# Sixteen exponential tiles, a V bank drawn per unit from all eight, one tile for gate and product, and a new order table

## The chip, the cores and the metric

The kernel runs on one core of a Trainium2 chip. The metric is the device time of one execution in microseconds (us). Before the change three runs took 1710.9, 1711.95 and 1711.96 us, so the median is 1711.95 us.

## What is computed

The input x has 2048 tokens of 512 numbers. It is normalised by a layer norm without weights to xn. One branch is full attention with 32 heads of 16 numbers each; the other is a bilinear gated feed-forward network of hidden width 1792. The output joins them.

```python
xn = layernorm(x)
q, k, v = split(xn @ wqkv)                     # 32 heads of 16
p = softmax(q @ k.T * 16 ** -0.5)              # 2048 x 2048 a head
s = (p @ v) @ wo
b = ((xn @ w_gate) * (xn @ w_up)) @ w_down     # 512 -> 1792 -> 512
out = x + s * silu(b)
```

All data are float32. Products other than p @ v split each operand into a high and a low float32r part and add three partial products, so they keep float32's precision.

## The kernel before, in words

**Units and steps.** Attention is cut into 32 units: eight groups of four heads (from line 887 on) by four chunks of 512 queries. A unit has 16 steps, one for each block of 128 keys. In a step `expo` (line 952) makes, for each of the four heads, one matmul of scores (128 keys by 512 queries, line 955) into a PSUM bank, and ScalarE (ACT) writes its exponentials to an SBUF tile `e` (line 957). When the four tiles of a step are there, `pv` (line 960) multiplies them with V (line 966): four matmuls of 128 rows by 32 columns, one for each head, each in a quarter of the bank `pv`, which adds up the 16 steps of its unit. Each of these float32 matmuls stands twice in the trace, so a step is eight records.

**Maxima.** The softmax needs each query's maximum over the keys. `score` (line 922) makes the scores a second time in the other layout (128 queries by 512 keys, line 927), and VectorE (DVE) reduces each bank to a maximum (line 929). There are 2048 such banks and 2048 of exponentials.

**Two halves of the array.** Score, exponential and all other products of the main part (the projections to q and k, gate, up, down and output products, line 465) use 48 to 64 rows of TensorE. A matmul in the lower half of the rows (0 to 63) runs beside one in the upper half. A product of 128 rows is done as a low part in the lower half and then a high part in the upper half; between them ACT reads one number of the bank (`look`, line 500), which holds the high part back until the low part has ended. The V products use all 128 rows and so have TensorE to themselves. A *batch* below is a run of V products without another matmul in it; a *stretch* is what stands between two batches.

**The order table.** The order on TensorE (PE), ACT and DVE is written out as a string, `ORDER`, and class `Order` (from line 470) reads it code by code:

- `t`/`T` one exponential, `s`/`S` one score block, each in the lower/upper half; the digit behind it is the PSUM bank
- `o` with a bank opens an output and makes its first low product, `f` makes a further low product, `F` a high product
- `v`, `w`, `z` one, two or three steps of V products
- `l` the look at a finished low part; `e` an output's copy by ACT, `d` one by DVE; `h` the split of a hidden block; `x`, `c`, `b` the three DVE pieces that read a unit's finished bank, divide by the sums and turn the result back; `m`, `r` the maxima of a unit; `k` the copies of turned tokens; `Q` the load of finished heads for the last product

Instructions that GpSimd (POOL) and the DMA queue (SP) get are put in order by the framework behind the mark `|`.

**Buffers.** `etile` (line 228) rotates through EBUFS = 14 tiles `e`, that is three and a half steps. PSUM has eight banks: seven with digits, and the eighth, tag `pv`, for the V products of every unit in turn. `pv` draws that bank anew where a unit begins (line 963), so the first V product of a unit waits until DVE has read the unit before (`first` in `heads`, line 993). The copies of q and k go through `qr` (three tiles, ACT writes, line 300) and `hl` (two tiles, POOL writes the high part, line 309); both are then stored to DRAM. In the feed-forward part ACT copies a gate block to `g` (line 683), DVE multiplies it with the up block into `h` (line 688), ACT writes the high part `hh` (line 434) and POOL the low part `hl` (line 435).

Of the kernel before, what the change touches and what calls it, by code (L numbers as in the profile page):

```python
# [41 lines left out]
2FfFfS5fFmfFfFfFs1Flo3S6efFfFs2FfFfFfFfFfS5fFfFfFrfS1o0FlfFs6FefFs2FfFfFs5FfFfFfS1fFfS6fFfFo4S2lfFs5FefFfFfFs1FfFfFs6F
fFfFfS2fS5fFo3FlfS1efFfT6s2Ft5T0fFfFfS1fS6t2Fs5FfFfT0fS1fFo2FlfT6s0FfT5fFs1FfFes6Ft0T5fFfFs1Ft4Fs6Ft0FfFfS5t1FfS4fFs6F
fS0et1T5lzs4T3s6Ft1Fo0FfT5s3FfT4fS1t6FfFfS5s3FfT4fFt6Fs1FfT5s4FfT3fS6fFt5S1lwet3S4s6T5t2Fo1FfFs3Ft4Fs5FfFt6S2fFfT3fS4f
T5fS6fFt2S3fFfFfFs4S5let2S6zo3T0s4FfT2fS5t6FfFs0Ft4FfS2t5FfFfT6s0FfFfS4fT5fT2s6FfFs0Flt5T4wemrt2S6s0Ft5Fo4FfT1fS2t6FfF
s0Fs5T1fFt2FfS6fFt1FfS0fT5fFfFfS6es2S1lt0S5wt3S6s2Ft0Fo1FfT5s3FfT6fFs2T0fFfT5fS3fT6fFs2T0fFt5Fs3FfFs6Fs2S0ewfT5o3S6lfT
4fS2fT0s5FfFt6Fs4Ft2Ft0FfFfT6s5FfFs4FfT2fFfT0s5FfS6s4S2elwxt0Fs5Ft1Ft6Fo4S2fT0fFfS5fT1fS6fT2fFfS0t5Fs1Ft6FfFfFs0Fs2S5e
fS1zlct6T3s0Ft2Fo5S1fFfT6fFfS0t3Ft1FfS2fFs6FfT0t3FfFfS2fT1fS6s0Fls3Fwes2T1t4T6s0Fo3FfFfS1fFfT2s0T4fFfS6t1FfT2fFt0S4fFs
6FfFfFs1Fls4T2t0Ft6Fwebt2S1t0Ft6Fs4Fo5FfT2fS1fFfT0fS4t6FfFt2S1fFt0FfS4fFmfS6es1S2zrfT0o4S6lfT3fS1fT2fFs0Ft6Ft3Fs1FfFt2
Fs0Ft6FfFs1T3fT2fFfS0fFt6T1fT3wels0T2o6T1fS3fFt5Fs2FfFfT0s3FfT1fS5t2FfFs0Ft3Fs1Ft5S2fFfFfS0efS3s1S5lzs2T4s0Ft3Fo1FfT5f  # L50
S4t2FfS3t0FfFs5Ft4FfT2s3FfFfS0fT4s5FfFfS3efS2t4T0lvxt6T4t0Fs5Ft3T2wct6S5t4S0t3Fo2FfFfS6fT5fS4fT0s3FfFfT6s5FfT4fFfFs3Ff
Fs5S0les6T4zs3T1o5T4t0S6fFfFfS1fT3s4FfT6fFt0Fs1FfFt3S4t6FfFs0FfT1fT3s4Ft6FwebfS0o1S4lfT3fFt6FfS2t0FfFs4Ft3FfS6t2Fs0FfF
t3S4fFfT6fFfFfS0es2T3lt4S6ws0T5s2Fo3T4fT6fFfS5fT0fS4mfFt2T6fFfS5s0Ft4FfFs2Ft6FfFfFs5Fls0S4et6Fzrt1S2s5Ft6Fo0T4fFfS1t2F
s6FfFfT5fS4fT1s2FfT6fT5fFs4FfFfT1wls2Fs4Fet6T5o1FfFfS3t2FfS6t4FfFfS5t3FfS2t6Fs4FfFfT3fFfFfS5es2T6ls4T3wxt0Fs5Ft6Fs2Ft3
Fs4Fo0Ft5FfS6t2FfFfS3fT5fS4fT6fFfFfS3efS2fS5t6T4lwct1S3s2T6t4Fo5FfFs1FfT3fS6fT2fFs4FfT1s3Ft6FfFfS2t1Fs4FfFfS3efS6s2S1l
zt0S4t3S6o2T1fFfFs0Ft4Fs3FfT6fFs1FfT0fT4s3FfFfS6fT0fT1fFt4Flbs3Ft0S6wet1S3t4Ft0Fo6S5fFfS1fT3fFfT4s5FfT0fT1s3FfFs4Ft5Fs
0FfFs3T1fFt5S4zdhmrfT1o0S3lfT5fS4fT2fFs1Ft3Ft5Fs4Ft2FfFs1FfFfT3fS4t5FfS2fFt3FfS1t4S5lwet3S2s1Ft4Fo5T6fFs3Ft2FfFfS1s4T6
fFfT3fS2fFfT6s1FfT4s3FfFfFs2S6lt4T1zdht4S3t1Fs2Fo6FfT0fS4fT3fS1fT2fS0fFfT4s3Ft1FfFfS2t4Fs0FfFs3Flt1Fs2T4vexs0T1s3Ft4Ft
5S2wct1S0s3T4t5Fo2FfFfS1fT0fS4fT3fS5fFt1FfS0fT4fFs3Ft1Fs5FfFs0T4lwdhs3T1s5T4t0Fo6FfFfS1fT3fS4t5FfFs0FfT1s3Ft4FfFs5Ft1T
0fFfS4fS3fFs5T1lzebt0S4t1T2o3S5fFfFfS0fT4fS1fT5fFs2FfT0s4Ft1FfFs5Ft0Fs2FfFt1T4fFs5S0lwds2T1t4T5s0Fo6FfFfS1fFfT2s0Ft4Ff  # L60
S5t1FfFfS2t0FfS4hmt5FfFs1FfS2fT0welrt5S4s1Ft0T3o2FfFfS5fT4s0FfT1fFs3Ft5Fs4Ft0FfS1fFfT5fFfS3s4FfS0s1T5lzdht5S3s4Ft0Fo1F
fT6fS5t3FfT0fS4fFfT6fS5t3FfFt0S4fFs6FfT5s3FfFt0Flt4s6S5wexs3T0t4Fs6T2o5FfFs0Ft3FfFt4Fs6FfT2fS0fT3fFs4FfT6fS2fT0fS3fFfS
4fFfS6s2S0lzcds3T4t6Fs2Fs0Ft1Fs4Ft3Ft6Fo2FfFt1FfS0fT3fT4fS6fFs1FfT0fT3fFfS6fT4fS1fFfFs0S3let6S4ws1T5t6Fs0Ft3Ft4Ft5Fs1F
t6Ft0Fwbs1T3o4T5s6FfFfT0fS3fT1fFfS6fT5fS0fT3fFs1Ft5FfS6fFfS0efT3s1S5lwmt2S6t3Fs0T1o5FfFs2FfT6s3FfT0fS1fFt2FfS6t3Ft0FfF
s1T2rfFfFs6FfFfFfS1efS3fS0s6S2lzt4S1t3Ft0S6o2FfFfS4fT1s3Ft6FfFfS0fT4t1Fs3FfT6fFt4S0fFfFs3T1fFs6Fls0Ft4Fhs3T1zes6T4s0Ft
1Ft5Ft3Fs4Fs6Ft1Fo0FfT5fT4fS3fFfS6fFt1Fs5FfT3fS4fT6vext1T3t6S5t2T4wcfS5fT1o3S6lfS2fT4fT5s1FfFt6Fs4FfFt5Fs2Ft6T1fFfFfS4
fFfS2fFs5S6ls1Ft4Fzdhs2T4t5Fs6Fs1Ft0Ft4Fo2FfS5fT6fT0fFfS1t4FfT5s6FfFfT0fFbfS1fT4s6S5lwes1T0s6Ft4Fs5Ft3Ft0Ft1Fo4FfS6fFf
S3fT5fS0fFfT1fS6fT5fFs3FfFs0S1lt5T6wds3T5t6T0s1Fo2FfFfS5fT3fFt6S1fS0mfFt5Ft3FfFfS1t6FhfS0t5FfFfFs1S3lwers0T6t5Fs1Ft4Ft
3Fs6Fo0FfS5fT1fFfS4fT6fT3fS5fFfS1t6Fs4FfFs5S3fFs1S6lzds4T5s3T1o6T2fFfFfS5fT4fFt1S3fFfT2fS5t4FfFs3T1fFt2Fhs5FfFt4Flt1Fw
ext2T4s3Fs5T1o0FfFfS2fFt3Fs4FfT5t1FfFs2FfT3fS4fT5fFfS1fFt3Fls2S4zcdhs1T5s2T3o4T6fFfFs5FfFt1Fs2T3fFfS6fT5s1FfFt2Ft3FfS6  # L70
fFfFfS1et5S2lt3S6wt0S1t5T3o2S6fFfFfS0fT1fS5fT6fFfT3s0FfFt1S5fT6fFs3Ft0FfS1fFfFs5Fls3Fs6Fs0T1zbdt1S5t3Fo6S0fT4fFs1Ft5Fs
# [1058 lines left out]
```

## Time and profile before

| what | value |
| --- | --- |
| median of three runs | 1711.95 us |
| the profiled execution, whole | 1711.76 us |
| its span, first to last instruction | 1708.6 us |
| PE busy | 1695.8 us (99%) |
| DVE busy | 1440.7 us (84%) |
| ACT busy | 1221.5 us (71%) |
| POOL busy | 583.7 us (34%) |
| DMA | 145.80 MB, mean 85 GB/s |

The profile is of one execution. Its span leaves out 3.2 us that lie around the first and last instruction. A row of a timeline gives start, duration, engine, line, operation, output<-inputs, shapes and how many instructions were merged into it; a bracket gives the idle time of the engine before it and what ended it. Matmuls are pipelined, so a matmul's row is longer than the distance to the next one; pace is read from starts.

### The profile page before, as it was taken

What the parts mean: (1) busy time and instruction counts of PE and PEld (TensorE: products, weight loads), DVE (VectorE), ACT (ScalarE), POOL (GpSimd) and SP (SyncE); (2) the same over time, 40 slices, a digit from 0 to 9 for tenths busy, and PEclk for the clock granted to TensorE, in tenths of its full rate; (3) what the DMA queues carried; (4) which work ended last, traced back from release to release, by engine and by line L of the source; (5) the groups of instructions that cost most, each with busy time, mean ns of one, the idle gap of its engine ahead of it and who ended that gap; (6) DMA issues with size and microseconds to landing.
All of it is one profiled execution on the core that took longest, in us unless ns stands there. A gap on an engine that the chain in (4) does not pass through costs nothing.

```text
span 1708.6 us, 35418 instructions
## 1 busy us (share of the span) xinstructions
PE 1695.8 (99%) x13792; PEld 1089.4 (64%) x13792; DVE 1440.7 (84%) x2464; ACT 1221.5 (71%) x2503; POOL 583.7 (34%) x618
## 2 busy tenths in 40 slices
...
PEclk9999999999999999999999999999999999999999
...
DMA packets 119794, 145.80 MB, mean 85 GB/s; under 512 B 12620, under 2 KB 74060, under 8 KB 116940
## 3 DMA queue, kind: packets, MB, share of 16 engines
...
## 4 chain that ended last, share of the span: by engine, by line
PE 97%; DVE 1%; POOL 1%; issue 0%; DMA 0%; ACT 0%; POOLq 0%; SPq 0%; DVEq 0%
PE b L465 37%; PE pv L966 27%; PE b L955 16%; PE b L927 15%; PE v L354 1%; PE p L354 0%; DVE mx L929 0%; DMA ks<-in_x_dram 0%; POOL dh L770 0%; PE b L332 0%; POOL y L441 0%; PE xT L317 0%; POOL hl L769 0%; ACT ks L295 0%; POOLq L1122 0%
## 5 line engine op out<-in xcount | busy, mean ns | idle before, releaser
L929 DVE TENSOR_REDUCE mx<-b 128x1 f32<-128x512 f32 x2048 | 1278.3, 683 | 186.4 <-PE b L927 99.3
L957 ACT ACTIVATE e<-b 128x512 f32<-128x512 f32 x2048 | 1084.1, 603 | 362.8 <-PE b L955 194.2
L927 PE MATMUL b<-ks,qs 48*128 48x512 f32 x2048 | 751.6, 412 | 0.0
L955 PE MATMUL b<-qs,ks 50*128 50x512 f32 x2048 | 722.4, 414 | 0.2
L966 PE MATMUL pv<-e,V 128*32 128x512 f32 x4096 | 488.4, 598 | 0.0
L955 PEld LDWEIGHTS b<-qs,ks 50*128 50x128 f32 x2048 | 342.4, 184 | 159.4 <-issue 48.6
L927 PEld LDWEIGHTS b<-ks,qs 48*128 48x128 f32 x2048 | 357.5, 184 | 131.6 <-DVE mx L929 51.0
L966 PEld LDWEIGHTS pv<-e,V 128*32 128x32 f32 x4096 | 109.0, 109 | 233.5 <-issue 223.6
L465 PE MATMUL b<-fh,w1h 64*128 64x512 f32 x504 | 199.4, 398 | 0.4 <-ACT look L500 0.4
L465 PE MATMUL b<-fl,w1h 64*128 64x512 f32 x504 | 197.4, 394 | 0.0
L465 PE MATMUL b<-fh,w1l 64*128 64x512 f32 x504 | 197.1, 393 | 0.0
L247 POOL CAST w1h<-w1r 128x512 fp32r<-128x512 f32 x60 | 36.6, 610 | 468.3 <-DMA w1r<-in_wg_dram 261.5
L465 PE MATMUL b<-fh,w0h 64*128 64x512 f32 x500 | 196.4, 395 | 0.0
L465 PE MATMUL b<-fl,w0h 64*128 64x512 f32 x500 | 195.7, 393 | 0.0
L465 PE MATMUL b<-fh,w0l 64*128 64x512 f32 x500 | 195.5, 393 | 0.0
L465 PE MATMUL b<-dh,hh 64*128 64x512 f32 x448 | 160.8, 396 | 0.0
L465 PE MATMUL b<-dh,hl 64*128 64x512 f32 x448 | 158.2, 394 | 0.0
L465 PE MATMUL b<-dl,hh 64*128 64x512 f32 x448 | 157.3, 393 | 0.0
L247 POOL CAST w0h<-w0r 128x512 fp32r<-128x512 f32 x60 | 36.6, 611 | 206.3 <-DMA w0r<-in_wu_dram 109.0
L465 PEld LDWEIGHTS b<-fh,w1h 64*128 64x128 f32 x504 | 92.9, 185 | 11.2 <-issue 2.2
L465 PEld LDWEIGHTS b<-fh,w1l 64*128 64x128 f32 x504 | 93.1, 185 | 8.8 <-issue 3.4
L465 PEld LDWEIGHTS b<-fl,w1h 64*128 64x128 f32 x504 | 93.3, 186 | 5.1 <-issue 0.8
...
## 6 DMA issues: line engine op xcount, KB each, us to landing
...
KD<-hl SPq DMA_DIRECT2D x16, 512.0 KB
QD<-hl SPq DMA_DIRECT2D x16, 512.0 KB
...
```

The costliest lines, as they stand in the source:

```text
L247: cast = nc.gpsimd.tensor_copy(hi, raw)
L354: nc.tensor.matmul(o, l(d), r(d), start=k == d == 0, stop=k == 2 and d == ND - 1)
L465: nc.tensor.matmul(self.o, l[rows], r[rows], start=x == 0 and n == 0, stop=last and (x == 0 or self.engine is not None), skip_group_check= ...
L927: nc.tensor.matmul(o, QS[i][b:b + KB, pr, t * P:(t + 1) * P], k[b:b + KB, pr, kc * 512:(kc + 1) * 512], start=True, stop=True)
L929: nc.vector.tensor_reduce(MX[i][:, j, t, kc:kc + 1], o, axis=AX.X, op=OP.max)
L955: nc.tensor.matmul(o, k[b:b + KR, pr, kt * P:(kt + 1) * P], QS[i][b:b + KR, pr], start=True, stop=True)
L957: fst["recent"] = fst["exp"] = nc.scalar.activation(e, o, AF.Exp, scale=DH ** -0.5).ins.name
L966: nc.tensor.matmul(fst["pv"][32 * j:32 * j + 32], V[:, kt, h0:h0 + 32], es[j], start=kt == 0, stop=kt == NT - 1)
```

## The change

The number of exponential tiles goes from 14 to 16, which is four whole steps. At the same time `qr` has two tiles in place of three, `hl` has one in place of two, and the product of gate and up block is written over the gate block, in tile `g`; tile `h` is gone. (At the very end `last_heads` took `h` for a low part; it now takes `e2`.)

The bank of V products is no longer a fixed one. A new code `P` with a digit draws any of the eight banks for the next unit and puts it in `pvs`; scores, exponentials and outputs may use digit 7 too. A unit's V products so write another bank than the one that DVE reads for the unit before, and a batch may hold the last steps of one unit and the first of the next.

The order table is written anew. A count over the two tables:

| | before | after |
| --- | --- | --- |
| steps of V products | 512 | 512 |
| batches of one, two, three steps | 40, 116, 80 | 11, 90, 107 |
| batches in all | 236 | 208 |
| stretches with 15 or more matmuls a half | 187 | 187 |
| shorter stretches | 49 | 21 |
| matmuls of the longer half, summed over the stretches | 4467 | 4461 |
| the same ahead of the first batch | 352 | 355 |

```diff
-EBUFS = 14
+EBUFS = 16
...
-fFfFfFfFfFs2FfFs5Flo3FfS1efS6fFfFfFfFs2FfFfFs5Fs1FfFfFfFo0S6lefS2fFfFfFs5FfFfFs1Fs6FfFfFfS2fFfF|o4S5lefS1fFfFs6FfFfFs
...
+t5S2lzdt3S6s7Ft5Fo2Ft1Fs3FfT6fFs7Ft5Fs1FfT3s6FfFfT5s7FfT1fFfS3s6T5fFfT7fFfS1fT5fS3t7S6lzds1T5t7S3o6T4fFfFfS5t1FfS7t3Fs
...
-        raw = qp.tile([P, D], F32, name="qr", bufs=3)
+        raw = qp.tile([P, D], F32, name="qr", bufs=2)
...
-            hi, lo = qp.tile([P, D], F32R, name="hl", bufs=2), raw.bitcast(F32R)
+            hi, lo = qp.tile([P, D], F32R, name="hl", bufs=1), raw.bitcast(F32R)
...
+                elif code == "P":
+                    pvs[len(pvs)] = pool(int(next(codes)))
...
-            fp = fst["fp"]
-            h = fp.tile([P, 512], F32, name="h", bufs=1)
-            nc.vector.tensor_tensor(h, o.o, gs[n], op=OP.mult)
+            h = gs.pop(n)
+            nc.vector.tensor_tensor(h, o.o, h, op=OP.mult)
...
-        tl = fp.tile([P, 512], F32, name="h", bufs=1).bitcast(F32R)
+        tl = fp.tile([P, 512], F32, name="e2", bufs=1).bitcast(F32R)
...
-        if kt == 0:
-            fst["pv"] = fst["banks"].tile([P, 512], F32, tag="pv", name=f"pv{i}", bufs=1)
...
-            nc.tensor.matmul(fst["pv"][32 * j:32 * j + 32], V[:, kt, h0:h0 + 32], es[j],
+            nc.tensor.matmul(pvs[i][32 * j:32 * j + 32], V[:, kt, h0:h0 + 32], es[j],
...
-        pv_bank = fst["pv"]
+        pv_bank = pvs[i]
```

The first place is on PE, where the sixth unit ends and the seventh begins. Before, with `pv_5530` the bank of the sixth unit and `pv_6225` that of the seventh, and L955 and L927 exponentials and scores:

```order
L966 MATMUL pv_5530<-e,V 32x512 x4
L955 MATMUL b_6202<-qs,ks_541 128x512
L955 MATMUL b_6206<-qs,ks_541 128x512
L955 MATMUL b_6210<-qs,ks_541 128x512
L927 MATMUL b_6214<-ks_541,qs 128x512
L955 MATMUL b_6217<-qs,ks_541 128x512
L955 MATMUL b_6221<-qs,ks_541 128x512
L966 MATMUL pv_6225<-e,V 32x512 x8
```

The same end of a unit on PE in the change (exponentials are now L956, scores L928, V products L965; `b_5420` is the sixth unit's bank):

```order
L928 MATMUL b_6047<-ks_541,qs 128x512
L956 MATMUL b_6050<-qs,ks_541 128x512
L956 MATMUL b_6055<-qs,ks_541 128x512
L956 MATMUL b_6059<-qs,ks_541 128x512
L965 MATMUL b_5420<-e,V 32x512 x12
L928 MATMUL b_6078<-ks_541,qs 128x512
L956 MATMUL b_6081<-qs,ks_541 128x512
L956 MATMUL b_6085<-qs,ks_541 128x512
L465 MATMUL b_5976<-dh,hh 128x512
```

Before, the last step of the unit stood alone, three matmuls a half later came two steps of the next; now three steps end the unit together, and a long stretch follows.

The second place is on PE at the end of the fourteenth unit in the change, where `b_11478` is its bank and `b_12180` that of the fifteenth, which a score block (`b_12160`, L928) used until seven matmuls before:

```order
L928 MATMUL b_12160<-ks_541,qs 128x512
L465 MATMUL b_12084<-fh,w0l 128x512
L956 MATMUL b_12164<-qs,ks_541 128x512
L928 MATMUL b_12168<-ks_541,qs 128x512
L465 MATMUL b_11987<-fh,w1l 128x512
L928 MATMUL b_12173<-ks_541,qs 128x512
L956 MATMUL b_12176<-qs,ks_541 128x512
L965 MATMUL b_11478<-e,V 32x512 x4
L965 MATMUL b_12180<-e,V 32x512 x4
L928 MATMUL b_12193<-ks_541,qs 128x512
```

One batch now holds steps of two units, in two banks.

The third place is on ACT, at the nineteenth hidden block: its high part (`hh`, L434), and the next gate copy (`g`). Before, the gate copy came nine rows later:

```order
L434 ACTIVATE hh<-h 128x512
L957 ACTIVATE e<-b_10291 128x512
L957 ACTIVATE e<-b_10304 128x512
L957 ACTIVATE e<-b_10311 128x512
L957 ACTIVATE e<-b_10325 128x512
L957 ACTIVATE e<-b_10333 128x512
L957 ACTIVATE e<-b_10342 128x512
L957 ACTIVATE e<-b_10353 128x512
L957 ACTIVATE e<-b_10363 128x512
L683 ACTIVATE g<-b_10183 128x512
```

In the change (L685 is the gate copy, L958 the exponentials):

```order
L958 ACTIVATE e<-b_10421 128x512
L434 ACTIVATE hh<-g 128x512
L958 ACTIVATE e<-b_10442 128x512
L958 ACTIVATE e<-b_10446 128x512
L685 ACTIVATE g<-b_10248 128x512
L958 ACTIVATE e<-b_10475 128x512
L500 ACTIVATE look<-b_10396 1x1
```

Two exponentials now stand between the two, and the gate copy writes the tile that POOL reads for the low part.

More of the change, by code (lines that the diff above doesn't have):

```diff
@@ L42 @@
[L42 to L71, printed above, removed]
@@ new lines @@
+FfFfFfS7mfFfFo3FlfFfFes1S6fS0fFfFfFfFfFfFs5FfS7fFo2FlfFfFrs1FefS6fFfFfFs0Fs5FfFs7FfFfFfS1fFs6S0ls5Fo4S7efFfFfFfFfFfFfF
+fFfS1fFfFs6Flo3FfFes0FfFt5S7t1FfFs6Ft2T0fS5fFfS7fS1fT6fT2fFs5Ft0FfFo7S6lfT2s1Ft0FfFfFes5Fs6T2s0FfFfT1fS4fT5fT2fFfFfS6s
+0Flt1Fs5Fs4Ft2Ft6FP1zet2S0o5S4fT6t3FfFfFfS0t2FfS4t6FfS3fFfT2s0Ft4T6fFfFfFs3S2ls0T4wes3T6s2T4o7T0fFfFs6Fs3Ft4Ft2FfS0fFt
+6Fs4Ft3FfFfS2fT0fFfS6fT3fS4s2T0lwes6T3s4S2t0T5vt3S6t0Fo4S5fFfT2fS3t6FfS0t5FfS2fFt3Fs6Ft0FfFs5Fs2T3fFfFfS6emfS0t3T5lzrs
+2T7o6T3fS0fT5fFs7Ft2FfS3t0FfS5fFt7Fs2FfT3fFfS0t7T5fFfFs2Fls3Ft7S0wet5S2s3T7t4Fo0FfFs5FfT2s7FfFt3Fs4FfT5fS2fT7fFfS3fT4f
@@ new lines @@
+FfFs2Fls5T7s3T4zexs2T7t4Fo5S3t6FfS1fFt7T2fFs4FfS3fFt6T1fFfS7fFfS4t2T6fFs3Fs7FfFt1S2lP4zecs3T6s7T1t0Fo2FfFs6Ft3FfS1t7Ff
+S0fFt6FfS3fT1fS7fFs0T6fFfS3s1FfFt6T7lwet6S0t7S3o1S5fFfFfT6fFt0T7s3FfFs6Ft5Fs0FfFt3FfS7fT6fFfS5s0T3fFs7T6lwebs5T3t6Fs0F
+t2Fs7Ft3Fo5FfFfS0fT6s2FfT7fFs3FfT6fS0t2T7fFfFfS3fS6t2S0lwems3T7t2T1s6S0wrs3T7o2T1fS6fFt0FfS7fFt3FfS6fT1s0Ft7Fs3FfFt6Ff
+S1t0S7fFfFfFt6T3ls1S0wet6S7t3T5o1Fs0FfFs6FfFfT7fS3t0FfS5fFt7Fs6Fs3T0fFfT5fS7fFfFt0T6ls3S5zexs7T0o3T6s5S2t4FfFt0FfFs7Ff
+T6fS5t4FfS2fFt0Fs7Ft6FfFs5S4fT0fT2fFfS6P7welcs5T0s4Fo2T1fFfT6s0FfT5fFs4Ft1Fs6FfT0fFfS5t1FfS4t6S0fFfFfFt1T5ls4S6zes0T1s
@@ new lines @@
+4Ft5Ft3Fs6Fo1FfS0fT5fS4fT3fFfT6fS5t0Fs3FfFfT4fFs6Ft0S5fFt4S3lwebt0S6t4Fs5Fo3Ft2Fs0FfT6s4FfT5fS2fFt0FfS6fT4fS5fFt0S2fFf
+FfFs6T4ls5T0wemrs2T4s6T0t1Fo5FfFs4Ft2FfFfS6t0FfS1t4FfS2fFfT0fS6fT1fFs4Ft0S2fFs6S1lzet0S4t3Fs2Ft6Fs1Fo0FfT4s3FfFfT2fS6f
+S1fT4fFt2S3fFt6Ft4FfT1fFfS2s3T6lwes2T4o1Fs3T6fFfS5fT4t2Fs6FfT3fFs4FfT5fS2t6FfFs3FfT4fFs5Fs2S6fFt4S3lP5zext4S2s6Ft0Fs3F
+t7Fs4Fo2Ft0FfFs6T7fFfT3fS0fT4fFfS7t6FfS3fS0fS4fFt6T7lzect6S3s0Ft7Fs4Fs1Ft6Fo3FfT7fFt0FfS6fT4fS7fT1s0FfFfT6fFfS4s7T1fFt
+6T0lwet1S4o7T6fS0fS2fFt1Ft4Fs6FfFt0Fs1Ft2FfFfS6fT4fS0fT1fFfFbs6Flt2S4s0T1zet2S6s4T1o3FfFfT0fS2fS6fT1fFfT4s0Ft2Fs1FfT6f
@@ new lines @@
+Fs4FfT0fFms2Flt6Fs1Fs4T0wert6S2t0Fs1Ft7Fo4Fs6FfFs2T0t1FfFfS7fS6fT0fFt2FfS1fT7fS0s6FfFfS2t1T7lzdhs0T1o6Ft7T2s3FfFfS1fT0
+fFfS7t3FfS2fT1s0FfFt3S7fFt2S1fFfFs0Flt3Ft2S7wexs1T3o0T2fS7fT4fS5fT3fS1fFt2Fs7FfFs5T4t3FfFs1Ft2FfFfS7t4Fs5FfFs3T2lP1zcd
+hs7T4o2Fs5T3fFt6Fs4FfT7fFfS5t3Fs6FfT4fFfS7t3FfS5fT6s4FfFt3S7fFt5S6lwet3S4s7Ft5Ft0Fo6FfS3t4FfFfS7fT5fS0fT3s4FfFs7T5fFs0
+T3fFfFs4FfT5t3S7lzbdhs0T5o4T3fS7t2FfFfS5fFfT0s7Ft3Fs2Ft5FfS0fFt7FfS3t2FfFfS5t7FfS0s3T2lwemrs5T7o2T6fS0fT3fFfS7t5Fs6FfT
+0s3FfFfT7fS5fFt0Fs6Ft7Fs3FfFs5S0fFt6T7lzdhs3T6s5Ft7Ft0Fs4Ft6Fo3FfS7fFs5T0fFfT4s6FfT7fFfS0fT5fFfFfS6et4S7lt5S0wt2S6t4Fs
@@ new lines @@
+7Ft5Fs0Ft2Fo6FfFs7FfT4fS5t0FfFfS2fT4fS7fT5fFfS0t4T2fFs7S5lP0zdhxt4S7o2S5fT3fFs1Ft4Ft7FfFs5FfT3fS4t1FfFfS7fT5s3FfT4s1Ff
+Ft5FfS7s3T4lwecs1T5s7T4o6Ft3FfFs5Ft1FfFfS7t4FfS3fS5t1FfFfT4fS7fS3fT1fFs5T4fFfT7fFs1ls3T4zds5T7s1Ft4Ft3Fs2Ft7Fo5FfS4fT1
+fFfS3fT2fS7fS4t1FfFt2S3fFfT7fFs1Ft2T4fFfFbfS3s7Fls1T2zemrt4S3t2Fs7Ft6Fs1Ft4Fo3FfS2t7FfS6fFs1T4fFt2FfFfS7fT4fS6s1T2fFfF
+fT4fFs7S2fS6fFs1T4lzes7T4s2Ft5Ft6Fs1Ft4Fo7FfFfS2t5FfS6t1FfFfS4s2T5fFfT6fS1fFs4T5fFfT2fS6fFfFs1T5lt2T4zexs6T5t2Fs1Fs0Ft
+4Fo3Ft5Fs6FfT2fFfS1fT4s0Ft5Fs6Ft2FfS4fT1fFs0FfT5fFhfS6s2S1fT4P5zelct4S0s6T7o2FfFfS1t4FfFfT0fS6t7Fs4Ft1FfS0fFfT6fS7t4Ff
@@ new lines @@
+FfS1s0Fls6Ft7T4wes1T7s0T4s6Fo3FfFt7FfFfT1fS0fS4t7FfFt6FfS1t0Ft7FfS4fS6fFfFs1T0lzbdht7S4s6Ft0Fs1Ft2Fo7FfFfT4fS6t0FfS2fT
+1fS4fFt6Fs0FfT2fS1fFt6S4fFs0T2lwemrs1T6s4Ft2Ft3Fs0Fs6Fo1FfT2fFs4T3fFfT0s2FfT6fS3fFt4FfFfT0dfS2fS6t4S3lzht0S7t4S2o6FfT3
+fFs0FfT7s4FfFs2T3fFfT0s7FfT4s3FfFt2FfFs0FfS7efS4t2T3lwt1S0s7Ft2Ft3Ft4Fs1Fo0FfS2fT7fS3fFt1S4fFfT2fT7fFs3S1fFs4T2fFfFt7S
+3lP2zdhxt7S1t4S3o6T5fFfFfS7fT1fS4fT3fFs5FfT7s1Ft4FfFs3Ft7T5fFfFcs1Fls4Ft7S3wes1T5t7Ft0Fs4Fs3Ft5Fo1FfFt7FfS4fS0fT3fFs5F
+fT7fT4fS3fFfFfS0s5T7lzdhs3T4o0T7fS5fFt6Fs4Ft3Fs7FfFt5S6fFt4FfS3fT7fS5fFt6FfFfT4bfS3t7Fls5S6wet4S3o7S5fT1fFfS6fT4s3Ft1F
```

195 lines of the change are left out of this document (97 added, 98 removed).

## The prediction, made before the result was known

> **What bounds the kernel now.** I read the page first: busy shares, the slices' clock, and the chain of work that ended last.
>
> ```profile
> span 1708.6 us, 35418 instructions
> PE 1695.8 (99%) x13792; PEld 1089.4 (64%) x13792; DVE 1440.7 (84%) x2464; ACT 1221.5 (71%) x2503; POOL 583.7 (34%) x618
> PEclk9999999999999999999999999999999999999999
> PE 97%; DVE 1%; POOL 1%; issue 0%; DMA 0%; ACT 0%; POOLq 0%; SPq 0%; DVEq 0%
> ```
>
> PE is busy nearly all the time at its full granted clock, and 97% of the chain is PE's. So time is won or lost only where PE's own sequence gets shorter or longer, or where another engine makes it wait. A busy share of 99% doesn't say that each matmul is at its best pace, so next I read PE's timeline where a unit ends, starts against starts.
>
> ```profile
> 406.38 0.39 PE L465 MATMUL b<-fh,w0l 64*128 64x512 f32 x1
> 406.50 0.40 PE L927 MATMUL b<-ks,qs 48*128 48x512 f32 x1
> 406.61 0.39 PE L465 MATMUL b<-fh,w0h 64*128 64x512 f32 x1
> 406.74 0.39 PE L955 MATMUL b<-qs,ks 50*128 50x512 f32 x1
> 407.06 1.06 PE L966 MATMUL pv<-e,V 128*32 128x512 f32 x8
> 408.05 0.73 PE L955 MATMUL b<-qs,ks 50*128 50x512 f32 x3
> 408.39 0.40 PE L927 MATMUL b<-ks,qs 48*128 48x512 f32 x1
> 408.62 0.41 PE L955 MATMUL b<-qs,ks 50*128 50x512 f32 x2
> 408.96 1.92 PE L966 MATMUL pv<-e,V 128*32 128x512 f32 x16
> 410.82 0.49 PE L465 MATMUL b<-fl,w0h 64*128 64x512 f32 x1
> 410.82 0.49 PE L927 MATMUL b<-ks,qs 48*128 48x512 f32 x1
> 411.15 0.39 PE L465 MATMUL b<-fh,w0l 64*128 64x512 f32 x1
> 411.16 0.39 PE L955 MATMUL b<-qs,ks 50*128 50x512 f32 x1
> 411.39 0.39 PE L465 MATMUL b<-fh,w1h 64*128 64x512 f32 x1
> ...
> 823.88 2.78 PE L966 MATMUL pv<-e,V 128*32 128x512 f32 x24
> 826.59 0.50 PE L955 MATMUL b<-qs,ks 50*128 50x512 f32 x1
> ```
>
> Three prices stand in these rows. **Pace:** matmuls of one half follow each other at 0.23 us (411.15 to 411.39; 406.38 to 406.61), the other half running beside them, so a pair costs 0.23 us. **V products:** from the batch's start to the next matmul a batch of one step takes 408.05 - 407.06 = 0.99 us, of two 410.82 - 408.96 = 1.86, of three 826.59 - 823.88 = 2.71. That is 0.86 us a step and some 0.135 us a batch, whatever its size. **Edges of a stretch:** the last pair before a batch takes 407.06 - 406.74 = 0.32 us and the first one after it 411.15 - 410.82 = 0.33, each 0.1 over the pace; the stretch of three pairs takes 408.96 - 408.05 = 0.91 us, 0.22 over three paces. I take 0.20. So **one batch more costs PE 0.135 + 0.20 = 0.335 us** beside its steps, though PE counts as busy all along.
>
> Then I check these prices against the whole main part, from the first batch to the last high product:
>
> ```profile
> 109.19 2.78 PE L966 MATMUL pv<-e,V 128*32 128x512 f32 x24
> ...
> 1698.29 0.39 PE L465 MATMUL b<-fh,w0l 64*128 64x512 f32 x1
> ```
>
> It lasts 1698.68 - 109.19 = 1589.5 us. By the counts of the order table: 512 steps x 0.86 = 440.3, 236 batches x 0.335 = 79.1, 4467 pairs x 0.23 = 1027.4, in all 1546.8 us. The other 42.7 us, 3%, are waits inside the stretches. Waits of PE's weight loads and of the two emptying engines show where they come from:
>
> ```profile
> PEld b L927 <- DVE mx L929: 51.0, 106, 0.8
> PEld b L955 <- ACT e L957: 43.6, 135, 1.0
> L929 DVE TENSOR_REDUCE mx<-b 128x1 f32<-128x512 f32 x2048 | 1278.3, 683 | 186.4 <-PE b L927 99.3
> L957 ACT ACTIVATE e<-b 128x512 f32<-128x512 f32 x2048 | 1084.1, 603 | 362.8 <-PE b L955 194.2
> 110.00:310.00 200.00, 200.00 (x1652) 126.87 (x1648) 166.48 (x282) 148.57 (x307) 68.08 (x74) 1.00 0.50 166
> 910.00:1110.00 200.00, 199.97 (x1637) 126.16 (x1635) 173.81 (x295) 150.37 (x307) 73.80 (x77) 1.00 0.22 61
> ```
>
> PE waits for a bank that DVE or ACT has not emptied yet, less than 1 us each time, and part of it is hidden, since weight loads run ahead. DVE is the nearer of the two: 173.8 us busy of 200 in the middle (third number pair of the windows), ACT 150.4. Still DVE is idle for 186 us before its reduces, most of it waiting for PE. It isn't the bound, but it has no more than an eighth to spare.
>
> **The change part by part.**
>
> *Batches.* 236 become 208: 28 x 0.335 = **-9.4 us**. Steps are the same 512, so their 440 us stay. All 28 stretches that go are short ones (49 to 21); 187 long ones stand in both tables. The short ones hold almost no waits: 0.91 us above is three paces and the two edges. So I leave the 42.7 us as they are, about 0.23 us for each long stretch, and nothing gained there.
>
> *Pairs.* Over the stretches the longer half has 6 matmuls less: 6 x 0.23 = **-1.4 us**. Ahead of the first batch it has 3 more: **+0.7 us**. The total of matmuls is the same.
>
> *Sixteen tiles.* The instructions are the same; with four steps of tiles, a batch of three leaves room for one step of exponentials while it runs (two of its four tiles with 14). ACT can go on over the batch, which could shorten waits on exponentials. From the rows above these are at most 43.6 us of weight loads' idle time, most of it hidden; I count 0, with 3 us as the gain at best.
>
> *The bank per unit.* No instruction is added; the wait of a unit's first V product goes from DVE's read of the unit before to the last reader of whatever bank it gets. In the order that reader is a reduce or an exponential whose matmul stands 6 to 17 places ahead. The tightest that open their batch have 8 or 9 places, 4 paces = 0.92 us, and the edge; the bank is free after a matmul's 0.39 us and a reduce of 0.68 or an exponential of 0.60, 1.0 to 1.1 us if the engine is idle. So it is 0.1 us short in about five units, more if DVE lags, and behind the waiting V product all of PE stands. Bounds: 0, and 31 units x 0.3 = 9 us; I take 0.5, near the lower end, since in most units 12 places or more lie between. Between the last step of one unit and DVE's `x`, two banks hold V products and six are left for everything else. [...]
>
> *Gate tile.* The next gate copy on ACT now waits until POOL has read the product for its low part.
>
> ```profile
> 677.36 0.63 ACT L434 ACTIVATE hh<-h 128x512 fp32r<-128x512 f32 x1 [1.64 <-DVE h L688]
> 678.07 1.30 POOL L435 TENSOR_TENSOR hl<-h,hh 128x512 fp32r<-128x512 f32 x1 [1.49 <-ACT hh L434]
> ```
>
> POOL ends 679.37 - 677.99 = 1.4 us after ACT's split when it is free. In the new order two gate copies have only two or three ACT instructions between (1.2 us: ACT waits 0.2 us), the others five or more. If a weight split of 1.9 us stands ahead on POOL, ACT waits 2 us, and the exponentials behind it with it; ACT has 29% to spare. Bounds 0 and 2 x 2 = 4 us; I take 0.5.
>
> *Fewer copies of q and k.* POOL's cast to the single `hl` must now wait until the store of the one before has landed, and ACT's copy until the store of the one two before has.
>
> ```profile
> 107.49 0.61 POOL L309 CAST hl<-qr 128x512 fp32r<-128x512 f32 x1
> 109.41 0.61 POOL L309 CAST hl<-qr 128x512 fp32r<-128x512 f32 x1
> 108.13 0.38 SPq L185 DMA_DIRECT2D KD<-hl  x1
> 93.04 0.57 SPq L177 DMA_DIRECT2D MD<-mt  x1
> 95.02 0.53 SPq L177 DMA_DIRECT2D qs<-MD  x2
> KD<-hl SPq DMA_DIRECT2D x16, 512.0 KB
> ```
>
> The landing isn't in the rows. A lower bound is the small store of maxima, whose reader is issued 1.98 us after it. An upper estimate adds 512 KB at that stretch's 166 GB/s, 3.1 us: 5.1 us. So a cast may follow the one before after 0.6 + 2.0 to 0.6 + 5.1 us, 2.6 to 5.7, where before it was 1.9. By the new table and the pace, copies come 7 us apart or more from about 104 us on, and that hides it; only four before that come 3 to 5 us after the one ahead, with a wait of 0 to 2.4 us each on POOL, in front of which ACT still has a second `qr`. Bounds 0 and 4 us; I take 0.5. In the SP queue the loads behind a late store wait as long; the queries among them are fetched a unit ahead.
>
> *The end.* What stands behind the last batch is the same; `e2` has long been read when `last_heads` takes it: 0.
>
> **Sum:** -9.4 - 1.4 + 0.7 + 0.5 + 0.5 + 0.5 = -8.6 us. The profiled execution took 1711.76 us, 0.2 below the median of the three runs. 1711.76 - 8.6 = 1703.2, or 1703.4 against the median. I forecast **1703.4 us**, 0.5% less. With all unknown waits at 0 and the 3 us of the tiles it is 1698.8; with 9, 4 and 4 at their upper ends, 1718, but not together, since most of these waits are the same idle time of PE.
>
> **The rivals.** *The emptying engines take the gain back.* After the change the same 2048 reduces must fit into 0.5% less time, and batches of three, in which DVE gets no new bank for 2.7 us, go from 80 to 107. If waits rise by 0.05 us in each of 187 long stretches, that is 9.4 us and nothing is left: about 1711.5 us. For it: DVE's 87% in the middle. Against it: DVE waits for PE far longer than PE for it.
>
> *The batches do not come off as ordered.* Twelve exponentials must be ready ahead of a batch of three; at 603 ns they are 7.2 us of ACT in a period of about 8.4 us. If each of the 27 added batches of three waits 0.17 us for its last tile, 4.6 us go: about 1707.8 us. For it: ACT's bank of the last exponential is ordered near the batch. Against it: the new order leaves more places between the last exponential and its V product than the old one.
>
> *Slower: the single `hl`.* From 93 to 275 us 26 copies pass through it. If a store takes so long under the other transfers that cast and store need over 7.1 us, the distance of the copies, every copy falls further behind, ACT stands at `qr`, and with it the exponentials and PE. At 7.6 us a copy it is 0.5 x 24 + 3 for the early ones = 15 us: 1711.8 - 10 + 15 = about 1717 us. It decides at a landing of 6.5 us. For it: DMA engines are busy for half of that stretch (0.50 in the window). Against it: 5.1 us by the estimate above.
>
> **How the numbers follow.** A measurement of this kernel can tell about 0.2%, 3.4 us, from no change; faster begins below 1708.5. Forecast 0.77, late batches 0.10 (faster too), emptying engines 0.09 (same), single `hl` 0.04 (slower). So faster 0.87, same 0.09, slower 0.04. The range goes from 1698.5, no unknown cost at all, to 1709, which takes in the late batches and 5 to 6 us of unknown waits; the last two cases lie outside with 0.13.
>
> **What would show it.** Right: V products again at 0.86 us a step and 0.135 a batch; PE's main part shorter by 10 us or so; idle times of PE's weight loads behind DVE and ACT no larger in sum. Wrong: more idle time on `PEld b L927 <- DVE mx`, V products that wait for a reduce or an exponential, ACT's `g` or `qr` with POOL or a DMA as releaser, or a first batch later than 110.5 us.

## The result and the profile after

The changed kernel takes **1721.8 us** (median of four runs, 1719.0 to 1724.0) against 1711.4 us before (four runs); the ratio is **1.006, 95% interval 1.0049 to 1.0072**. It is slower by 0.6%, where 0.5% faster was forecast, and it lies 13 us above the range.

The page of the changed kernel, the lines that answer to those of before:

```profile
span 1718.7 us, 35300 instructions
PE 1696.9 (99%) x13792; PEld 1089.6 (63%) x13792; DVE 1424.5 (83%) x2464; ACT 1233.2 (72%) x2503; POOL 583.8 (34%) x618
PE 94%; DMA 2%; POOL 1%; DVE 1%; ACT 1%; issue 0%; SPq 0%; POOLq 0%; DVEq 0%
```

The busy shares hardly move, but PE's part of the chain falls from 97% to 94%; DMA has 2% of it now. PE's busy time grew by only 1.1 us of the 10.1 that the span got longer; the rest is time in which PE stands. PE's timeline shows where, with a V batch of one, two and three steps and what follows it, and the first and the last row of the main part:

```profile
115.67 2.78 PE L965 MATMUL b<-e,V 128*32 128x512 f32 x24
...
299.43 1.04 PE L965 MATMUL b<-e,V 128*32 128x512 f32 x8
300.40 0.50 PE L928 MATMUL b<-ks,qs 48*128 48x512 f32 x1
...
305.88 1.93 PE L965 MATMUL b<-e,V 128*32 128x512 f32 x16
307.74 0.49 PE L928 MATMUL b<-ks,qs 48*128 48x512 f32 x1
...
313.17 2.78 PE L965 MATMUL b<-e,V 128*32 128x512 f32 x24
315.88 0.50 PE L928 MATMUL b<-ks,qs 48*128 48x512 f32 x1
...
1708.28 0.39 PE L465 MATMUL b<-fh,w0l 64*128 64x512 f32 x1
```

The batches still cost 0.97, 1.86 and 2.71 us. But the main part begins at 115.67 us, 6.5 later than before (109.19), and lasts 1708.67 - 115.67 = 1593.0 us, 3.5 longer, where the counts alone make it 10.8 shorter. So 6.5 us went into the opening, of which the prediction had counted 0.7, and some 14 us of new waits into the main part. The list of waits names the engines (us in total, times, longest):

```profile
PEld b L956 <- ACT e L958: 43.5, 183, 0.8
PEld b L928 <- DVE mx L930: 28.5, 72, 0.8
PEld b L956 <- ACT g L685: 19.0, 21, 1.8
ACT g L685 <- POOL hl L435: 10.2, 4, 3.8
POOL hl L309 <- DMA KD<-hl: 8.7, 4, 3.6
POOL hl L309 <- DMA QD<-hl: 6.3, 2, 4.7
```

Weight loads wait less for DVE's reduces than before (28.5 against 51.0 us) and as long for exponentials (43.5 against 43.6). But these are two rows of many: summed over the whole list, weight loads wait 96.2 us for DVE (98.6 before) and 111.9 for ACT (99.7 before). For ACT's gate copies alone they wait 19.0 us, 5.0 before. New is that the gate copy itself waits for POOL. The rows of three places with new waits follow. First the opening (timeline of ACT; the bracket holds the wait and its releaser):

```profile
27.96 0.60 ACT L300 ACTIVATE qr<-xT 128x512 f32<-128x512 f32 x1 [1.64 <-POOL xl L310]
30.63 0.60 ACT L300 ACTIVATE qr<-xT 128x512 f32<-128x512 f32 x1 [2.07 <-POOL xl L310]
38.66 0.60 ACT L336 ACTIVATE qr<-b 128x512 f32<-128x512 f32 x1 [1.61 <-POOL xl L340]
```

Then one of three stalls in the middle, ACT and POOL:

```profile
694.47 0.62 ACT L434 ACTIVATE hh<-g 128x512 fp32r<-128x512 f32 x1
...
696.63 0.61 POOL L247 CAST w0h<-w0r 128x512 fp32r<-128x512 f32 x1 [7.47 <-DMA w0r<-in_wu_dram]
697.32 1.27 POOL L250 TENSOR_TENSOR w0l<-w0r,w0h 128x512 fp32r<-128x512 f32 x1
698.56 1.27 POOL L435 TENSOR_TENSOR hl<-g,hh 128x512 fp32r<-128x512 f32 x1
...
699.87 0.60 ACT L685 ACTIVATE g<-b 128x512 f32<-128x512 f32 x1 [3.80 <-POOL hl L435]
```

ACT split the product at 694.47, but POOL took it up only at 698.56: ahead of it in POOL's queue stood the split of a weight block that was still on its way from DRAM. Until then the tile `g` isn't free, and ACT stands for 3.80 us with the exponentials behind it. Last the end of the main part, PE and SP:

```profile
1645.19 0.56 SPq L177 DMA_DIRECT2D MD<-mt  x1
1645.81 0.75 SPq L177 DMA_DIRECT2D hh<-in_x_dram  x1
1649.56 0.33 SPq L177 DMA_DIRECT2D hh<-YD  x1
1649.94 0.59 SPq L177 DMA_DIRECT2D qs<-MD  x2
...
1654.16 0.70 PE L956 MATMUL b<-qs,ks 50*128 50x512 f32 x3 [2.91 <-DMA qs<-MD]
1654.79 3.12 PE L965 MATMUL b<-e,V 128*32 128x512 f32 x16
```

The last unit's exponentials wait 2.91 us for their maxima, whose load stands behind two loads of 512 KB. The V batch after it takes 3.12 us in place of 1.92; the windows view shows why (the column ahead of the last two is the granted clock):

```profile
0.00:50.00 50.00, 43.00 (x251) 32.66 (x252) 31.01 (x85) 28.81 (x53) 30.78 (x40) 0.93 0.54 179
1640.00:1662.00 22.00, 19.09 (x134) 8.28 (x133) 5.08 (x12) 15.86 (x34) 0.34 (x1) 0.92 0.49 155
```

A mean of 0.92 over 22 us is 1.7 us lost (in windows of 1 us it reads 0.50 from 1656 to 1658 us, and 1.00 again from 1659 on), and 0.93 over 50 us some 3.5 us. Before, both windows showed 1.00:

```profile
0.00:50.00 50.00, 44.36 (x299) 34.66 (x301) 34.96 (x86) 30.67 (x58) 33.52 (x44) 1.00 0.59 192
1640.00:1662.00 22.00, 22.00 (x167) 10.09 (x165) 4.87 (x8) 20.18 (x44) 7.79 (x8) 1.00 0.31 106
```

Over the whole span the mean granted clock is 0.996, and 0.999 before. That is some 5 us, half of what the span got longer.

### The profile page after: what moved, and what is told of

Its sections match the earlier page's. It is cut to its first block, busy times and chain, and to the rows that moved or that the text cites. A ratio compares the mean times of both kernels' runs of the same rounds, so it can differ in the third digit from the quotient of the medians.

```text
span 1718.7 us, 35300 instructions
## 1 busy us (share of the span) xinstructions
PE 1696.9 (99%) x13792; PEld 1089.6 (63%) x13792; DVE 1424.5 (83%) x2464; ACT 1233.2 (72%) x2503; POOL 583.8 (34%) x618
## 4 chain that ended last, share of the span: by engine, by line
PE 94%; DMA 2%; POOL 1%; DVE 1%; ACT 1%; issue 0%; SPq 0%; POOLq 0%; DVEq 0%
PE b L465 36%; PE b L965 26%; PE b L928 15%; PE b L956 15%; DMA wdr<-OD 1%; DVE mx L930 0%; PE p L354 0%; DMA w0r<-in_wu_dram 0%; PE v L354 0%; DMA out_dram<-hh 0%; ACT e L958 0%; DMA out_dram<-dl 0%; DMA ks<-in_x_dram 0%; DMA OD<-tr 0%; POOL w0l L250 0%
## 5 line engine op out<-in xcount | busy, mean ns | idle before, releaser
L930 DVE TENSOR_REDUCE mx<-b 128x1 f32<-128x512 f32 x2048 | 1261.2, 681 | 198.8 <-PE b L928 107.0
L958 ACT ACTIVATE e<-b 128x512 f32<-128x512 f32 x2048 | 1095.1, 601 | 342.2 <-PE b L956 190.6
L928 PE MATMUL b<-ks,qs 48*128 48x512 f32 x2048 | 754.5, 412 | 1.2 <-ACT g L685 1.2
L956 PE MATMUL b<-qs,ks 50*128 50x512 f32 x2048 | 747.0, 416 | 6.3 <-DMA qs<-MD 2.9
L965 PE MATMUL b<-e,V 128*32 128x512 f32 x4096 | 483.8, 598 | 0.0
L928 PEld LDWEIGHTS b<-ks,qs 48*128 48x128 f32 x2048 | 359.8, 185 | 148.0 <-DVE mx L930 28.5
L956 PEld LDWEIGHTS b<-qs,ks 50*128 50x128 f32 x2048 | 349.2, 185 | 153.9 <-ACT e L958 43.5
L965 PEld LDWEIGHTS b<-e,V 128*32 128x32 f32 x4096 | 112.0, 109 | 238.6 <-issue 232.7
L465 PE MATMUL b<-dl,hh 64*128 64x512 f32 x448 | 160.9, 393 | 0.0
```

The source lines that it names most:

```text
L465: nc.tensor.matmul(self.o, l[rows], r[rows], start=x == 0 and n == 0, stop=last and (x == 0 or self.engine is not None), skip_group_check= ...
L928: nc.tensor.matmul(o, QS[i][b:b + KB, pr, t * P:(t + 1) * P], k[b:b + KB, pr, kc * 512:(kc + 1) * 512], start=True, stop=True)
L930: nc.vector.tensor_reduce(MX[i][:, j, t, kc:kc + 1], o, axis=AX.X, op=OP.max)
L956: nc.tensor.matmul(o, k[b:b + KR, pr, kt * P:(kt + 1) * P], QS[i][b:b + KR, pr], start=True, stop=True)
L958: fst["recent"] = fst["exp"] = nc.scalar.activation(e, o, AF.Exp, scale=DH ** -0.5).ins.name
L965: nc.tensor.matmul(pvs[i][32 * j:32 * j + 32], V[:, kt, h0:h0 + 32], es[j], start=kt == 0, stop=kt == NT - 1)
```

## The experiments

The theory after the two traces: three separate stalls, from the fewer `qr` and `hl` tiles, from the gate tile and at the end, hide a gain of about 10 us. The rivals: the emptying engines bind and every stall only moves on, or fewer batches are worth less than counted. Medians are of 4 to 10 runs, beside runs of the kernel before on the same chip.

| run | median, us | ratio to before, 95% | first batch, us |
| --- | --- | --- | --- |
| the change | 1721.8 | 1.0049 to 1.0072 | 115.67 |
| e1_product_in_e2 | 1743.0 | 1.0167 to 1.0194 | 116.37 |
| e2_raws_in_e | 1722.1 | 1.0047 to 1.0072 | 114.82 |
| e3_maxima_first | 1716.7 | 1.0017 to 1.0040 | 114.53 |
| e4_all_three | 1740.2 | 1.0150 to 1.0177 | 116.27 |
| e5_all_raws_in_e | 1717.6 | 1.0019 to 1.0039 | 111.75 |
| e6_product_mostly_e2 | 1716.3 | 1.0013 to 1.0032 | 114.42 |
| **e7_three_mended** | **1707.3** | **0.9965 to 0.9984** | 111.07 |
| b8_before_few_qr | 1717.3 | 1.0020 to 1.0039 | 113.31 |
| b9_before_over_gate | 1762.3 | 1.0280 to 1.0312 | 109.62 |
| e10_forty_batches_more | 1719.2 | 1.0034 to 1.0062 | 110.60 |

The first batch is read from one trace of each kernel. e3 and e6 leave the opening as it is in the change, and yet theirs comes 1.1 and 1.2 us earlier. One reason shows in the clock: over the first 50 us its mean is 0.93 in the trace of the change and 0.97 in that of e3, which is 2 us, and the change reads 0.91 already in the first 20 us, before any wait on `qr`. For e6 no such window is on record. So a difference of about 1 us in that column can be chance.

**The product in another tile (e1).**

```diff
-            h = gs.pop(n)
-            nc.vector.tensor_tensor(h, o.o, h, op=OP.mult)
+            h = fst["fp"].tile([P, 512], F32, name="e2", bufs=1)
+            nc.vector.tensor_tensor(h, o.o, gs[n], op=OP.mult)
```

> Against the changed kernel's 1721.8 us median. The product of gate and up goes into the tile e2 (free but for the four silus of a chunk), so the gate tile is free again as soon as DVE has read it; everything else stays as in the changed kernel. Theory (the gate tile held through POOL's subtraction stalls ACT): the three PE gaps of 1.55 to 1.74 us at 573, 699 and 800 us vanish and with them the smaller waits on g; 5 to 7 us less, 1715 to 1717 us. Rival (ACT and DVE can't empty banks fast enough for the new order, and the stall only takes the name of g): under 1.5 us less, 1720 or more.

It is 21 us slower still, a miss on both sides. The gaps at 573, 699 and 800 us are gone, and larger ones stand where a chunk's silus use the same tile `e2` (timeline of DVE and POOL):

```profile
631.06 0.62 POOL L440 TENSOR_SCALAR e<-e 128x512 f32<-128x512 f32 x1
631.76 1.26 POOL L441 TENSOR_TENSOR y<-e,y 128x512 f32<-128x512 f32 x1
633.06 0.69 DVE L689 TENSOR_TENSOR e<-b,g 128x512 f32<-128x512 f32 x1 [3.85 <-POOL y L441]
```

The silu's pieces wait on POOL as the hidden block did, behind a weight split. So the place of the stall is right, and the mend was bad: it tied DVE to POOL's queue instead of ACT.

**Raw copies of the opening elsewhere (e2).** The raw copies of the four turns and of four of eight X copies lie in exponential tiles, which idle there.

```diff
-        raw = qp.tile([P, D], F32, name="qr", bufs=2)
+        raw = qp.tile([P, D], F32, name="qr", bufs=2) if hi is None else etile()
...
-            raw = qp.tile([P, D], F32, name="qr", bufs=2)
+            raw = etile() if tt < 12 else qp.tile([P, D], F32, name="qr", bufs=2)
```

> Against 1721.8 us. In the opening the raw copies of the four layer-norm turns and of the first four X copies go into exponential tiles, which are idle there; the other X copies and all projections keep the two qr tiles and the single hl. Theory (two qr tiles make ACT wait for POOL's splits): the first batch comes at 110 to 111 us in place of 115.7, and the PE gap of 1.3 us at 38.7 with the half-clock window behind it goes; 4 to 6.5 us less, 1715 to 1718 us. Rival (it is the single hl, or the new order's own opening): first batch after 114 us, under 2 us less.

No change, and the rival's number. But the timeline of ACT shows that the waits had only moved to the copies that still used `qr`:

```profile
44.81 0.60 ACT L300 ACTIVATE qr<-b 128x512 f32<-128x512 f32 x1 [2.98 <-POOL xl L340]
46.72 0.60 ACT L336 ACTIVATE qr<-b 128x512 f32<-128x512 f32 x1 [1.31 <-POOL xl L340]
50.56 0.60 ACT L336 ACTIVATE qr<-b 128x512 f32<-128x512 f32 x1 [2.73 <-POOL xl L340]
```

POOL needs 0.61 + 1.29 us for each copy and works them off one by one; the copies that ACT makes faster only wait later. So the run didn't decide between the two, and e5 was made.

**Maxima ahead of the side loads (e3).**

```diff
-            dma(QS[i][row:row + 2].bitcast(F32), md[e])
+            put = dmar(QS[i][row:row + 2], md[e].bitcast(F32R))
+            if i == NU - 1:
+                fst["maxed"] = put.ins.name
...
-                dma(here[:, 0:2], YD[c][:, t:t + 2])
-                dma(here[:, 2:4], x[(4 * c + t) * P:(4 * c + t + 2) * P].rearrange("(t p) d -> p t d", p=P))
+                for sl, src in ((slice(0, 2), YD[c][:, t:t + 2]),
+                                (slice(2, 4), x[(4 * c + t) * P:(4 * c + t + 2) * P].rearrange("(t p) d -> p t d", p=P))):
+                    put = nc.sync.dma_start(here[:, sl], src)
+                    if "maxed" in fst:
+                        tc.add_manual_dep(put.ins, fst["maxed"], BEHIND, reason="behind the last unit's maxima")
```

> Against 1721.8 us. The last unit's maxima are read back (qs<-MD) ahead of the two side loads into hh that stand before them on SP's queue; no other instruction moves. Theory (the maxima sit on SP's queue behind a load that waits for the landing of out_dram<-hh): the PE gap of 3.3 us at 1650.9 and the half-clock window behind it (1.7 us) go; 3 to 5 us less, 1717 to 1719 us. Rival (the wait is the maxima's own way through DVE and DRAM, or the end is bound elsewhere): under 1 us less.

5.1 us less, just above the 3 to 5 expected. The timeline of SP and PE corrects the reason:

```profile
1645.87 0.56 SPq L177 DMA_DIRECT2D MD<-mt  x1
1651.36 0.58 SPq L185 DMA_DIRECT2D qs<-MD  x2
1653.25 0.34 SPq L836 DMA_DIRECT2D hh<-YD  x1
...
1653.36 0.71 PE L961 MATMUL b<-qs,ks 50*128 50x512 f32 x3 [0.96 <-DMA qs<-MD]
```

The load of the maxima is issued 5.5 us after their store, not sooner than before the edit (4.75 us): no load of `hh` stands between the two now, so the store itself lands late (SP waits 4.9 us for it). What got shorter is the way from issue to use: 2.0 us, where it was 1654.16 - 1649.94 = 4.2 us with the two big loads just ahead. PE's wait is 1.95 us shorter, and the half-clock window behind it (1.7 us) is gone: the clock is 1.00 from 1640 to 1662 us. The other 1.4 us these rows don't place; the opening, which the edit leaves alone, came 1.1 us sooner in this trace, and the runs of the change alone spread over 5 us.

**The three together (e4).**

> Against 1721.8 us, with the edits of the three other kernels together. Theory (three separate stalls hide a gain of about 10 us from fewer batches): the savings add to 13 to 18 us, 1704 to 1709 us, below the kernel before (1711.4), with batches still 11, 90 and 107 of one, two and three steps. Rival (fewer batches are worth less than counted, or the emptying engines bind): 1712 us or more.

1740.2 us, far outside the 1704 to 1709 expected: the bad mend of e1 is in it, and it says nothing on the sum.

**All raw copies elsewhere (e5).** The last four X copies go into the tiles of the four turns.

```diff
+            raw = etile()
+            spare.append(raw)
...
+            raw = etile() if tt < 12 else spare.pop(0)
```

> Against 1721.8 us. All twelve raw copies of the opening (four layer-norm turns, eight X copies) now lie in exponential tiles; qr and hl serve the projections alone. In the run with eight of them moved, ACT still waited 2.98, 1.31 and 2.73 us for POOL's subtractions where the last X copies use qr, and the first batch came at 114.8. Theory (too few qr tiles tie ACT to POOL's queue): the first batch comes at 109.5 to 111.5 us, 3.5 to 6 us less, 1716 to 1718.5 us. Rival (the new order's opening, with the single hl, is late by itself): first batch at 113.5 or later, under 2 us less.

4.3 us less; the first batch comes 3.9 earlier than in the change (2.7 earlier than in e3 and e6), just outside the interval given, and no raw copy of ACT waits for POOL. The tiles are the cause of most of the late opening; with 111.75 where 109.9 was counted, 1.9 us of it are left unexplained.

**The same fewer tiles in the kernel before (b8).**

```diff
-name="qr", bufs=3
+name="qr", bufs=2
...
-name="hl", bufs=2
+name="hl", bufs=1
```

> Against the kernel before, 1711.4 us: that kernel with two qr tiles and one hl in place of three and two, nothing else (fourteen exponential tiles, the old order, the old bank, h as it was). Theory (these fewer tiles make the opening late): the first batch moves from 109.2 to 113 to 116 us, 4 to 7 us more, 1715 to 1718 us. Rival (the new order makes it late): under 1.5 us more, first batch before 111.

5.6 us more in the old order too, first batch at 113.31, 4.1 later. So the fewer tiles make the opening late without the new order. Which part of it is `qr` and which the single `hl` was not taken apart here; e5 left `hl` single and got 4.3 us back.

**The product in e2 only where no silu runs (e6).**

```diff
-            h = gs.pop(n)
-            nc.vector.tensor_tensor(h, o.o, h, op=OP.mult)
+            h = gs[n] if c and f < 3 else fst["fp"].tile([P, 512], F32, name="e2", bufs=1)
+            nc.vector.tensor_tensor(h, o.o, gs.pop(n), op=OP.mult)
```

> Against 1721.8 us. The product goes into e2, except for the first three hidden groups of chunks 1 to 3, where the four silus hold e2 and it stays over the gate tile. In the run with every product in e2 the gaps at 573, 699 and 800 us were gone, and gaps of 1.3 to 6.3 us stood where the silus run. Theory: without both, waits in the windows from 500 to 800 us fall from 4.2, 4.2 and 3.9 us to 2.4 to 2.8 each, 4 to 6 us less in all, 1715.5 to 1718 us. Rival (the stalls move on to the next tile of the chain): under 1.5 us less.

5.5 us less. By the prediction's prices, the waits in the stretches that begin between 500 and 800 us fall from 13.1 us in the change to 8.2, and no gap of the size of those stalls stands elsewhere in the middle; ACT's gate copies wait 0.6 us for POOL in all, against 10.2. Weight loads still wait 15.1 us for gate copies (19.0 in the change, 5.0 before). So most of that wait isn't POOL's, and this run leaves it in.

**The kernel before with its product over the gate tile (b9).** The diff is the change's own at that place, alone.

> Against the kernel before, 1711.7 us: that kernel with its product written over the gate tile (no tile h), nothing else. Theory (the next gate copy then waits for POOL's subtraction behind whatever weight split stands ahead of it, in any order of this kind): 2 to 7 us more, 1714 to 1719 us, with PE gaps over 1 us that have g behind them. Rival (only the new order puts the gate copy so close behind the split of the hidden group): under 1 us more.

**50.7 us more**, seven times the upper end expected. In the old order the gate copy comes nine rows behind the split of the hidden block, and waits all the same (timeline, ACT and POOL):

```profile
1312.08 0.63 ACT L434 ACTIVATE hh<-g 128x512 fp32r<-128x512 f32 x1
...
1315.49 0.61 POOL L247 CAST w0h<-w0r 128x512 fp32r<-128x512 f32 x1 [5.40 <-DMA w0r<-in_wu_dram]
1316.18 1.26 POOL L250 TENSOR_TENSOR w0l<-w0r,w0h 128x512 fp32r<-128x512 f32 x1
1317.38 0.61 POOL L647 CAST dh<-wdr 128x512 fp32r<-128x512 f32 x1
1318.07 1.26 POOL L648 TENSOR_TENSOR dl<-wdr,dh 128x512 fp32r<-128x512 f32 x1
1319.29 1.26 POOL L435 TENSOR_TENSOR hl<-g,hh 128x512 fp32r<-128x512 f32 x1
...
1320.59 0.60 ACT L683 ACTIVATE g<-b 128x512 f32<-128x512 f32 x1 [7.36 <-POOL hl L435]
```

A load that is still under way, two splits of 1.9 us each and the subtraction stand in front: 7.36 us. ACT's gate copies wait 46.8 us for POOL in twelve such waits; the new order has only four. PE stands 28.4 us for these gate copies, and some 23 us more are clock: the mean granted clock of this execution is 0.986, where 0.999 stood before. So nine rows of distance on ACT are no protection. In these rows it is what stands ahead of the subtraction in POOL's queue that counts; no run moved the subtraction there.

**The three mends in one (e7)**: e3, e5 and e6.

> Against 1721.8 us and the kernel before's 1711.4: the two edits above and the maxima ahead of the side loads (5.1 us less alone). Theory (three stalls of their own hide the gain of fewer batches): the savings add, 13 to 17 us less, 1705 to 1709 us, faster than before. Rival (they overlap or give way to one another, or the fewer batches are worth less than 0.335 us each): 1711 us or more.

**1707.3 us, 14.5 less than the change and 0.25% (0.16 to 0.35%) less than before.** The savings of the three alone sum to 5.1 + 4.3 + 5.5 = 14.9 us, so they add within the spread of the runs. The page and PE's timeline:

```profile
span 1705.4 us, 35344 instructions
PE 1690.2 (99%) x13792; PEld 1087.5 (64%) x13792; DVE 1427.9 (84%) x2464; ACT 1232.3 (72%) x2503; POOL 583.7 (34%) x618
...
111.07 2.78 PE L974 MATMUL b<-e,V 128*32 128x512 f32 x24
...
1695.04 0.39 PE L469 MATMUL b<-fh,w0l 64*128 64x512 f32 x1
```

The main part takes 1695.43 - 111.07 = 1584.4 us, 5.1 less than before. This version beats both kernels.

**Forty batches more (e10)**, made from the kernel with the three mends; in forty places of its order a batch of three steps is cut:

```diff
-P1zet2S0o5S4fT6
+P1wet2S0vo5S4fT6
```

This is the first of the forty places: `z` becomes `w`, and `v` follows after a pair.

> Against the mended kernel with three edits, 1707.3 us: forty of its batches of three steps are split into two steps, one pair of other products, and one step; everything else as it was (248 batches in place of 208). Theory (each batch costs 0.137 us more for the same steps and about 0.20 us at the edge of a stretch): 40 x 0.335 = 13.4 us more, 1719 to 1722.5 us. Rival (the edges are hidden: only the batches' own 0.137 us count): 5.5 us more, 1712 to 1714 us. Second rival (the number of batches doesn't set the time): under 2 us more.

11.9 us more, 0.30 a batch. Main parts give the same: 1596.3 against 1584.4 us. The price is nearly the 0.335 of the prediction, and the edges are not hidden. (The added stretches are of one pair each.)

## Why the prediction was wrong

The step that failed is the pricing of three waits. The sum put them at 0.5 us (fewer copies of q and k), 0.5 us (the gate tile) and 0 (the end); taking them back gave 4.3, 5.5 and 5.1 us. The gain by batches was there, and these waits hid it.

*Batches: right.* -9.4 us for 28 batches stood on 0.335 us each; e10 measured 0.30, which makes it -8.3, and the batches keep their prices in the change. *Pairs: not tested alone.* Nothing in the rows speaks against them, and a step costs 0.86 us as before.

*Fewer copies of q and k: mis-sized, and the wrong customers.* I took 0.5 us, at most 4, and looked only at the stores of projections. The layer-norm turns and the X copies of the opening use `qr` too, twelve copies of 1.9 us each on POOL; with two tiles ACT stands behind POOL there. Measured: 4.3 us back in e5, 5.6 us more in b8; a part of it is clock: the first 50 us run at 0.93 in the change and at 1.00 in e7, which has e5's edit, and the mean clock is 0.993 to 0.997 in the runs of the change and 0.996 to 0.999 in those of e5. The term stood for the right tile and the wrong work. The mark that I had set, a first batch later than 110.5 us, was the sign.

*Gate tile: mis-sized.* I took 0.5 us and at most 4, from the number of ACT instructions between split and gate copy and from a POOL that has at most one weight split ahead. Measured: 5.5 us in e6. ACT's distances don't set the wait alone, as b9 shows with 50.7 us at nine rows' distance; the rows put it down to what stands ahead of the subtraction in POOL's queue. At 694 us in the change, and in b9's row, that was a split whose load was still on its way from DRAM; at 573 and at 800 us it was two splits of 1.9 us each, where I had allowed for one. The row that I quoted showed POOL when it was free; I should have read what stands ahead of `hl` in POOL's queue at every hidden block.

*The end: wrong.* I wrote 0, looking only behind the last batch. The new order brings the last unit's maxima so close to their use that 4.2 us of loading stand on PE's path: 5.1 us in e3, its half-clock window among them.

*The clock: left out.* No term of the sum has it. Beside the stalls, half of what the change lost in its profiled execution is clock (0.996 against 0.999 before), and the spread of its runs goes with it (0.997 in the run of 1719.0 us, 0.993 in that of 1724.0).

*The bank per unit and sixteen tiles: no large cost seen.* The V batches of the change hold 1.2 us beyond their prices, all in the batch at half clock, so no V product waited for its bank or its tiles within a batch. The weight loads of V products waited 4.1 us in eleven waits for DVE's read of the unit before; in the change they wait 3.7 us in eleven waits for reduces, at most 0.4 each. So the wait went to another reader, as predicted, and stayed small. Neither part was taken back by itself.

*Waits left as they are: not quite.* By the prices of the prediction the mended kernel (e7) has 48.3 us of waits inside stretches against 42.7 before; 3.2 us of the difference stand after 1500 us, where PE still waits 0.9 us for the last maxima and 0.6 us for finished heads. These 5.6 us and the 1.2 us of a first batch at 111.07, where 109.9 was counted, are more than the 1.5 us that I had allowed for unknown waits; the forecast of 1703.4 lies 3.9 below the 1707.3 measured. What each of these waits is was not tried. (The upper end of my sum, with 9, 4 and 4 us, is 1719 us and not 1718.)

*The rivals.* Emptying engines: they did not take the gain back, since it came once the three stalls were mended. But my sign for being right, waits no larger in sum, did not hold: in the mended kernel weight loads wait 96.1 us for DVE and 108.8 for ACT, 6.6 us more than before. Late exponentials: not borne out; weight loads of V products wait 1.8 us in all for exponentials in the change. The single `hl`: the outcome was on its side, the mechanism not; POOL waits for the landing of a store six times, 15.0 us in all, at most 4.7 us, ACT once behind it, 1.0 us, and most later copies find POOL waiting for ACT, so no queue grows.
